# The output projection of a fused retention and SwiGLU kernel as seven products of halves, with its weight blocks streamed from DRAM

## The chip, the cores and the metric

One core of a Trainium2 chip runs the whole kernel. The metric is the device time of one execution, in microseconds. Where two kernels are compared by a ratio, it is the mean time of the one kernel's runs over the mean time of the other's runs of the same rounds on the same chip. It is therefore not quite the ratio of the medians that are quoted beside it.

The engines are called by the names of the profile: PE is TensorE (matmuls), PEld its weight loads, DVE is VectorE, ACT is ScalarE, POOL is GpSimd. SP is SyncE, which here does nothing but issue DMA transfers; SPq is its queue.

## The reference, cut to what matters

```python
# q, k, v: (8, 8, 576, 64).  Attention with decay, then, per token (4608 of them, 512 wide):
x   = ret(q, k, v)                                   # (4608, 512)
xn  = x / sqrt(mean(x*x) + 1e-6) * rms_g
g   = xn @ w_gate                                    # 512 -> 1536
val = xn @ w_val
out = (g * sigmoid(g) * val) @ w_out                 # 1536 -> 512, float32
```

The last product, with `w_out`, is the output projection, and it is what the change rewrites.

## The kernel before

The tokens are worked through in 12 tiles of 384 (`u` = 0 to 11). Tiles 0 and 1 belong to a start phase, in which the weights are also brought into float32. From tile 2 on, each tile consists of six steps of `up` (the two up projections, already written as seven products of halves, a Strassen scheme), then the output projection `down`. Attention for later tiles ("slots") and the norm of the next tile stand between them.

```python
    def down(u, s):                       # three times a tile, 128 tokens each
        ps = bank(f"out_{u}_{s}")
        for f in range(NF):               # 12 blocks of d_ff
            nc.tensor.matmul(
                ps[:, :DM], lhsT=h_of[u][:, f, s * P : s * P + P], rhs=w_out[:, f],
                start=(f == 0), stop=(f == NF - 1),
            )
        o = o_all[:, (u * (NS) + s) % 2]
        nc.scalar.copy(out=o, in_=ps[:, :DM])
        nc.sync.dma_start(out=out[u * U + s * P : u * U + s * P + P, :], in_=o)
    ...
    SLOTS = (((0, 2, 4, 5), 5), ((6,), 9), ((1, 3, 5), 10))

    def behind(u, i):                     # a slot, and the three steps of the next tile's norm
        at, n = SLOTS[u % 3]
        if i in at:
            j = u // 3 * 8 + n + at.index(i)
            slot(j)
            following(j)                  # transposes for j+1, then 13 loads for j+2
        if u + 1 < NU and 5 <= i < 8:
            (norm_0, norm_1, norm_2)[i - 5](u + 1)

    with tc.manual_schedule():            # every engine keeps this program order
        start()                           # ends with: down(0, s) and norm_s(2) in turn, slot(9)
        for u in range(2, NU):
            for i in range(2 * NG):
                for _ in up(u, i % 2, i // 2):
                    pass
                behind(u, i)
            for s in range(NS):
                down(u, s)
                behind(u, 2 * NG + s)
```

The last step of the norm, `norm_2`, scales x, and then forms four differences of quarters of x for the seven products:

```python
        for o, a, b in ((t3, b22, b12), (b12, b12, b11), (t2, b22, b12), (t4, b21, t2)):
            nc.vector.tensor_tensor(out=o, in0=a, in1=b, op=ALU.subtract)
```

Of the kernel before, what the change touches and what calls it, by code (L numbers as in the profile page):

```python
# [10 lines left out]
F32 = mybir.dt.float32  # L11
U32 = mybir.dt.uint32
AF = mybir.ActivationFunctionType
ALU = mybir.AluOpType
P = 128
# [27 lines left out]
def kernel(  # L43
# [11 lines left out]
    nc = tc.nc  # L55
    B, H, S, D = q.shape
    NTOK, DM = out.shape
# [6 lines left out]
    SQ = 32  # L64
    U = 384
    HU = U // 2
    NS = U // P
    NU = NTOK // U
    NH = NF // 2
    NG = NH // 2  # L70
# [5 lines left out]
    const = ctx.enter_context(tc.tile_pool(name="const", bufs=1))  # L76
# [2 lines left out]
    xp = ctx.enter_context(tc.tile_pool(name="xp", bufs=3))  # L79
    ffn = ctx.enter_context(tc.tile_pool(name="ffn", bufs=1))  # L80
    tmp = ctx.enter_context(tc.tile_pool(name="tmp", bufs=6))
    PS = bass.MemoryType.PSUM
    trio = ctx.enter_context(tc.tile_pool(name="trio", bufs=1, space=PS))
    banks = ctx.enter_context(tc.tile_pool(name="banks", bufs=5, space=PS))

    def bank(name):
        return banks.tile([P, 512], F32, tag="b", name=name)

    def temp(name):
        return tmp.tile([P, U], F32, tag="t", name=name)  # L90
# [17 lines left out]
    tick = const.tile([1, 1], F32, name="tick")  # L108
    rms_g = const.tile([P, NHP], F32, name="rms_g")
    w_out = const.tile([P, NF, DM], F32, name="w_out")  # L110
    o_all = const.tile([P, 2, DM], F32, name="o_all")



# [5 lines left out]
    A11, A12, S1, A22, S2, S3, S4 = range(7)  # L120
# [6 lines left out]
    x_of, t_of, h_of = {}, {}, {}  # L127
# [3 lines left out]
    def load_qk(j):  # L131
        b, hp = jobs[j]
        for nm, src in (("q", q), ("k", k)):

            t = raw.tile([P, S // SQ, SQ], F32, tag=nm + "raw", name=f"{nm}raw_{j}")
            for e in range(2):
                rows = src[b, 2 * hp + e].rearrange("(t b) (i a) -> i b t a", b=SQ, a=SQ)
                for i in range(D // SQ):
                    r = e * D + i * SQ
                    nc.sync.dma_start(out=t[r : r + SQ], in_=rows[i])  # L140
            st[j][nm + "raw"] = t
# [20 lines left out]
    def load_kv(j):  # L162

        b, hp = jobs[j]
        for nm, src, bufs in (("k", k, 4), ("v", v, 3)):
            if nm in st[j]:
                continue
            t = raw.tile([P, NFULL, 2, D], F32, tag=nm, name=f"{nm}_{j}", bufs=bufs)
            for e in range(2):
                nc.sync.dma_start(  # L170
                    out=t[:, :, e],
                    in_=src[b, 2 * hp + e, : NFULL * P].rearrange("(c p) d -> p c d", p=P),
                )
            st[j][nm] = t
        t = st[j]["vt"] = raw.tile([L, 2, D], F32, tag="vt", name=f"vt_{j}", bufs=3)
        nc.sync.dma_start(
            out=t, in_=v[b, 2 * hp : 2 * hp + 2, NFULL * P :].rearrange("e p d -> p e d")
        )
# [22 lines left out]
    def prepare(j):  # L201

        d = st[j]
        for nm in ("q", "k"):
            t = att.tile([P, S], F32, tag=nm + "T", name=f"{nm}T_{j}")
            nc.vector.transpose(out=t, in_=d.pop(nm + "raw").rearrange("p t a -> p (t a)"))
            d[nm + "T"] = t
        scale_v(j)
# [143 lines left out]
    def following(j):  # L352
        if j + 1 < len(jobs):
            prepare(j + 1)
        if j + 2 < len(jobs):
            load_qk(j + 2)
            load_kv(j + 2)
# [140 lines left out]
    def down(u, s):  # L498
        ps = bank(f"out_{u}_{s}")
        for f in range(NF):  # L500
            nc.tensor.matmul(  # L501
                ps[:, :DM], lhsT=h_of[u][:, f, s * P : s * P + P], rhs=w_out[:, f],
                start=(f == 0), stop=(f == NF - 1),
            )
        o = o_all[:, (u * (NS) + s) % 2]
        nc.scalar.copy(out=o, in_=ps[:, :DM])  # L506
        nc.sync.dma_start(out=out[u * U + s * P : u * U + s * P + P, :], in_=o)



    chunks = []
    for g in range(NG):
        for m, src in enumerate((moe_w_gate, moe_w_val)):
            for half in range(2):
                n = (half * NH + 2 * g) * P
# [87 lines left out]
    def combine(m):  # L603
        for g in range(NG):
            w = w_up[m][:, :, 2 * g * P : 2 * g * P + 2 * P]
            for o, a, b, op in (
                (S3, A11, A21, ALU.subtract), (S1, A21, A22, ALU.add),
                (S2, S1, A11, ALU.subtract), (S4, A12, S2, ALU.subtract),
            ):
                o, a, b = (w[:, 2 * n : 2 * n + 2] for n in (o, a, b))  # L610
                nc.gpsimd.tensor_tensor(out=o, in0=a, in1=b, op=op)

    def weights_to(n):

        nonlocal n_chunks
        while n_chunks < min(n, len(chunks)):
            mantissa(n_chunks + 1)
            join(n_chunks)
            load_chunks(n_chunks + 4)
            exponent(n_chunks + 2)  # L620
            n_chunks += 1
# [3 lines left out]
    def start():  # L625

        h_of[0] = ffn.tile([P, NF, U], F32, tag="h", name="h_0")
        tables = list(zip((causal, gv, gc, gq), (_causal_table(), *_decay_tables(H, D))))

        def table(i):  # L630
            t, values_ = tables[i]
            src = nc.inline_tensor(values_, name=t.tensor.name + "_table")
            nc.scalar.dma_start(out=t, in_=src.ap())

        make_identity(nc, ident)
        nc.vector.memset(ones, 1.0)
        for j in range(NHP):
            load_first(j)
            if j + 1 < NHP:
                load_kv(j)  # L640
        for i in (1, 0, 2):
            table(i)
        load_chunks(2)
        table(3)
        nc.scalar.dma_start(out=rms_g, in_=moe_rms_g.rearrange("(c p) -> p c", p=P))
        load_chunks(3)
        turn(0)
        sq = []
        for j in range(NHP):
            slot(j)  # L650
            if j + 1 < NHP:
                turn(j + 1)
            if j:
                sq.append(square(0, j - 1))
            if j == 0:
                exponent(0)
                exponent(1)
            elif j == 1:
                load_kv(NHP - 1)
                mantissa(0)  # L660
                weights_to(1)
                load_qk(NHP)
            elif j == 2:
                weights_to(2)
                load_kv(NHP)
        values(NHP - 1)
        carried(NHP - 1)
        sq.append(square(0, NHP - 1))
        norm_0(0, sq)
        norm_1(0)  # L670
        norm_2(0)
        following(NHP - 1)
        step = 0
        order = [(0, 0, 0), 4, (0, 1, 0), 5, (0, 0, 1), 6, (0, 1, 1), 7, (0, 0, 2)]
        order += [(1, 0, 0), (1, 1, 0), (0, 1, 2)]
        order += [(1, m, g) for g in (1, 2) for m in range(2)]
        for what in order:
            if not isinstance(what, tuple):
                slot(what, rest=what > NHP)
                following(what)  # L680
                if what == 2 * NHP - 1:
                    values(what)
                    carried(what)
                    norm_0(1)
                    norm_1(1)
                continue
            u, m, g = what
            weights_to(4 * g + 2 * m + 2)
            for _ in up_plain(u, m, g):
                step += 1  # L690
                weights_to(2 + (step + 1) // 2)
            if what == (0, 0, 2):
                norm_2(1)
        weights_to(len(chunks))
        combine(0)
        for u in (1, 0):
            for s in range(NS):
                down(u, s)
                if u == 0:
                    (norm_0, norm_1, norm_2)[s](2)  # L700
            if u:
                combine(1)
                slot(8, rest=False)
                following(8)
        slot(9)
        following(9)



    SLOTS = (((0, 2, 4, 5), 5), ((6,), 9), ((1, 3, 5), 10))  # L710

    def behind(u, i):
        at, n = SLOTS[u % 3]
        if i in at:
            j = u // 3 * 8 + n + at.index(i)
            slot(j)
            following(j)
        if u + 1 < NU and 5 <= i < 8:
            (norm_0, norm_1, norm_2)[i - 5](u + 1)

    with tc.manual_schedule():
        start()
        for u in range(2, NU):
            for i in range(2 * NG):
                for _ in up(u, i % 2, i // 2):
                    pass
                behind(u, i)
            for s in range(NS):
                down(u, s)
                behind(u, 2 * NG + s)  # L730


# [25 lines left out]
```

## Time and profile before

| | before |
|---|---|
| median of the first 3 runs | 1227.73 us (1227.61 to 1229.58) |
| span of the profiled run | 1226.5 us, granted clock 0.986 |
| TensorE busy | 1175.6 us, 96% |
| VectorE busy | 567.0 us, 46% |
| output projection on TensorE, one tile | 72 instructions of 512 columns, 30.9 us |
| one tile from the end of `up` to the next `up` (u=2) | 35.0 us, without a hole |

The page gives the totals. The chain of work that ended last says which of them count, and the timeline of one stretch, read engine by engine, says why. The prediction below shows those lines and how they are read.

### The profile page before, as it was taken

The numbers are of one execution on the slowest core, as the hardware profiler recorded it, in microseconds if no ns is written. First come the engines' busy times: TensorE is split into PE (matmuls) and PEld (weight loads), VectorE is DVE, ScalarE is ACT, GpSimd is POOL, SyncE is SP. The second block draws the span as 40 slices with busy tenths as digits, with TensorE's granted clock in tenths as the row PEclk, the third lists the DMA queues.
The fourth block names the chain that finished last, engine by engine and source line by source line (L and its number), as shares of the span: only waits on it lengthen the run. The fifth ranks groups of instructions, "written<-read, shape, count | busy, mean of one in ns | idle before, by whom it ended". The sixth has DMA issues, their size and how long they took to land.

```text
span 1226.5 us, 21417 instructions
## 1 busy us (share of the span) xinstructions
PE 1175.6 (96%) x9224; PEld 894.6 (73%) x9224; DVE 567.0 (46%) x1216; ACT 257.5 (21%) x488; POOL 45.2 (4%) x74
## 2 busy tenths in 40 slices
PE   4697899999999999999999999999999999999998
PEld 3455555447976985976985994985994995894993
DVE  3888871024643662433562663343563463342340
ACT  4554550012111120121220211211220220120110
POOL 0000004130000000000000000000000000000000
PEclk9799799999999999999999999999999999999999
DMA  8588420022240331002221242002122200000000
GB/s 219 118 209 202 122 99 1 18 64 47 44 80 18 62 72 46 1 9 56 39 51 51 40 76 55 9 1 59 33 50 55 47 2 18 9 1 18 9 1 26
DMA packets 224526, 65.52 MB, mean 53 GB/s; under 512 B 212016, under 2 KB 212144, under 8 KB 224432
## 3 DMA queue, kind: packets, MB, share of 16 engines
q1 hardware_dynamic: 215360, 45.12, 18.0%
q10 hardware_dynamic: 9072, 19.05, 4.7%
q8 instruction: 72, 1.18, 0.4%
q14 instruction: 22, 0.18, 0.0%
HBM read 54.70 MB, written 9.44 MB: 52 GB/s over the span
## 4 chain that ended last, share of the span: by engine, by line
PE 87%; DVE 1%; ACT 0%; issue 0%; POOL 0%; ACTq 0%; DVEq 0%; POOLq 0%
PE out L501 30%; PE x L430 13%; PE z L430 13%; PE w L430 13%; PE y L430 6%; PE up L487 6%; PE av L316 2%; PE av L297 1%; PE s L235 1%; PE s L255 1%; PE rb L397 1%; PE ms L377 0%; DVE x L399 0%; DVE w_val L597 0%; DVE sum L280 0%
## 5 line engine op out<-in xcount | busy, mean ns | idle before, releaser
L501 PE MATMUL out<-w_out,h 128*128 128x512 f32 x792 | 346.3, 594 | 0.0
L501 PEld LDWEIGHTS out<-w_out,h 128*128 128x128 f32 x792 | 149.0, 190 | 177.9 <-issue 175.1
L437 DVE TENSOR_TENSOR u<-m,y 128x384 f32<-128x384 f32 x60 | 32.7, 545 | 141.4 <-PE y L430 141.4
L506 ACT COPY o_all<-out 128x512 f32<-128x512 f32 x36 | 21.1, 586 | 366.3 <-PE out L501 348.4
L430 PE MATMUL z<-x,w_gate 128*128 128x192 f32 x480 | 87.9, 326 | 2.2 <-DVE sum L280 2.2
L430 PE MATMUL x<-x,w_val 128*128 128x192 f32 x480 | 88.8, 328 | 0.0
L430 PE MATMUL x<-x,w_gate 128*128 128x192 f32 x480 | 88.5, 328 | 0.0
L430 PE MATMUL w<-sums,w_gate 128*128 128x192 f32 x480 | 87.8, 326 | 0.0
L430 PE MATMUL z<-x,w_val 128*128 128x192 f32 x480 | 87.8, 326 | 0.0
L430 PE MATMUL w<-sums,w_val 128*128 128x192 f32 x480 | 87.8, 326 | 0.0
L430 PEld LDWEIGHTS x<-x,w_gate 128*128 128x128 f32 x480 | 79.5, 190 | 4.8 <-issue 4.3
L430 PEld LDWEIGHTS z<-x,w_gate 128*128 128x128 f32 x480 | 79.6, 190 | 2.5 <-DVE sum L280 2.5
L430 PEld LDWEIGHTS w<-sums,w_val 128*128 128x128 f32 x480 | 79.7, 190 | 0.0
L430 PEld LDWEIGHTS w<-sums,w_gate 128*128 128x128 f32 x480 | 79.7, 190 | 0.0
L430 PEld LDWEIGHTS z<-x,w_val 128*128 128x128 f32 x480 | 79.6, 190 | 0.0
L430 PEld LDWEIGHTS x<-x,w_val 128*128 128x128 f32 x480 | 79.2, 190 | 0.6
L454 ACT COPY m<-x 128x384 f32<-128x384 f32 x60 | 28.7, 479 | 202.9 <-PE x L430 202.9
L487 PE MATMUL up<-x,w_gate 128*128 128x384 f32 x192 | 68.3, 515 | 3.2 <-DVE x L399 1.5
L437 DVE TENSOR_TENSOR h<-u,w 128x384 f32<-128x384 f32 x60 | 33.3, 554 | 76.4 <-PE w L430 76.4
L268 DVE SCALAR_TENSOR_TENSOR ret<-s,causal 128x320 f32<-128x320 f32 x64 | 28.4, 486 | 86.8 <-PE last L255 49.8
L399 DVE SCALAR_TENSOR_TENSOR x<-x,rms_g,rb 128x384 f32<-128x384 f32 x48 | 26.3, 610 | 86.6 <-PE rb L397 86.6
L449 ACT ACTIVATE h<-h 128x384 f32<-128x384 f32 x90 | 47.0, 523 | 88.6 <-DVE h L437 88.6
(99 smaller groups left out, 1332.7 us busy)
## 6 DMA issues: line engine op xcount, KB each, us to landing
out_dram<-o_all SPq DMA_DIRECT2D x36, 256.0 KB, 2.0
k<-in_k_dram SPq DMA_DIRECT2D x64, 128.0 KB, 3.0
v<-in_v_dram SPq DMA_DIRECT2D x64, 128.0 KB, 2.8
qraw<-in_q_dram SPq DMA_DIRECT2D x112, 72.0 KB, 2.5
kraw<-in_k_dram SPq DMA_DIRECT2D x112, 72.0 KB, 2.6
w_out<-in_moe_w_gate_dram ACTq DMA_DIRECT2D x6, 1024.0 KB, 6.8
w_out<-in_moe_w_val_dram ACTq DMA_DIRECT2D x3, 1024.0 KB, 5.7
w_gate<-in_moe_w_val_dram ACTq DMA_DIRECT2D x3, 1024.0 KB, 6.1
```

What stands on the lines that cost most here:

```text
L235: nc.tensor.matmul(s[side(odd), e, i * L : i * L + L], lhsT=d["kT"][side(e), c * L : c * L + L], rhs=d["qT"][side(e), c * L : c * L + L], ...
L255: nc.tensor.matmul(o[side(e)], lhsT=d["k"][side(odd), i, e], rhs=d["v"][side(odd), i, e], start=True, stop=True,)
L268: nc.vector.scalar_tensor_tensor(out=ret[:, e], in0=s[:, e, :SC].rearrange("p (c k) -> p c k", k=L), scalar=float(_gamma(H)[2 * hp + e] ** ...
L316: mm = nc.tensor.matmul(av[odd][side(e), i * L : i * L + L], lhsT=d["sum"][side(e), c - 1], rhs=d["qT"][side(e), c * L : c * L + L], start ...
L399: nc.vector.scalar_tensor_tensor(out=x[:, c], in0=x[:, c], scalar=rms_g[:, c : c + 1], in1=rb[:, :U], op0=ALU.mult, op1=ALU.mult,)
L430: nc.tensor.matmul(ps[:, i * HU : i * HU + HU], lhsT=w_up[m][:, 2 * blk + c, cut], rhs=t_of[u][blk][:, c], start=(start and i == c == 0), ...
L437: nc.vector.tensor_tensor(out=o, in0=a, in1=pairs_of(ps), op=ALU.add)
L449: nc.scalar.activation(out=o, in_=c, func=AF.Silu)
L454: nc.scalar.copy(out=s1, in_=pairs_of(x_))
L487: nc.tensor.matmul(ps[:, :U], lhsT=w_up[m][:, 4 * half + c, i * P : i * P + P], rhs=x_of[u][:, c], start=(c == 0), stop=(c == NHP - 1),)
L501: nc.tensor.matmul(ps[:, :DM], lhsT=h_of[u][:, f, s * P : s * P + P], rhs=w_out[:, f], start=(f == 0), stop=(f == NF - 1),)
L506: nc.scalar.copy(out=o, in_=ps[:, :DM])
```

## The change

The intent is to save an eighth of the output projection's TensorE work. With d_model on the output partitions, the product of a 512x1536 and a 1536x384 matrix is cut into halves each way, and seven products of halves replace eight. This needs sums of blocks of `w_out` (formed once, on GpSimd), sums of blocks of h (four on VectorE for each tile), seven weight blocks where the tile of `w_out` holds four (so all seven are kept in DRAM and streamed through four slots), and a transposition of the results on the way out (VectorE, in 32x32 blocks; each result then leaves in eight stores with rows of 128 bytes).

```diff
+    w_blocks = dram.tile([7, P, NH, DH], F32, name="w_blocks")
+    w_slots = w_out.rearrange("p f d -> p (f d)").rearrange("p (s f d) -> p s f d", s=4, d=DH)
...
+    def combine_out():
+        a11, a12, a21, a22 = (quarter(r, c) for r in range(2) for c in range(2))
+        for o, a, b, op in (
+            (a22, a21, a22, ALU.add), (a21, a11, a21, ALU.subtract),
+            (a11, a22, a11, ALU.subtract), (a12, a12, a11, ALU.subtract),
+        ):
+            nc.gpsimd.tensor_tensor(out=o, in0=a, in1=b, op=op)
...
+    def fetch():                          # one block from DRAM into the slot that came free
+            nc.sync.dma_start(
+                out=w_slots[:, n_fetched % 4], in_=w_blocks[ORDER[n_fetched % 7]]
+            )
...
+    def across(u):
...
+        def product(rhs, ps, start):      # 12 matmuls of 192 columns, then a fetch
...
+        block(t1, b12, b11, ALU.subtract)
+        block(b12, b22, b12, ALU.subtract)
+        yield                             # the slot and norm_0 stand here
+        product(b11, x_, True)
+        ...
+        yield
+        product(t1, z, True)
+        yield                             # norm_1 here
+        product(b12, w, True)
+        yield
+        product(b11, y, True)
+        add(u2, s1, y); add(u4, u2, z); result(1, 1, u4, w)
+        yield                             # norm_2 here
+        product(b21, x_, False); result(0, 0, None, x_); block(b21, b21, b11, ALU.subtract)
+        yield
+        product(b22, z, False);  result(0, 1, u2, z)
+        yield
+        product(b21, w, False);  result(1, 0, u2, w)
...
         slot(9)
         following(9)
+        return combine_out()
-    SLOTS = (((0, 2, 4, 5), 5), ((6,), 9), ((1, 3, 5), 10))
+    SLOTS = (((0, 2, 4, 5), 5), ((5,), 9), ((1, 3, 5), 10))
```

The stores of the four sums and the first four fetches are issued behind the third `up` step of tile 2. Tiles 0 and 1 keep `down`.

More of the change, by code (lines that the diff above doesn't have):

```diff
@@ L81 @@
     tmp = ctx.enter_context(tc.tile_pool(name="tmp", bufs=6))
+    outs = ctx.enter_context(tc.tile_pool(name="outs", bufs=3))
     PS = bass.MemoryType.PSUM
+    dram = ctx.enter_context(tc.tile_pool(name="dram", bufs=1, space=bass.MemoryType.DRAM))
     trio = ctx.enter_context(tc.tile_pool(name="trio", bufs=1, space=PS))
@@ L110 @@
     w_out = const.tile([P, NF, DM], F32, name="w_out")
-    o_all = const.tile([P, 2, DM], F32, name="o_all")
     A11, A12, S1, A22, S2, S3, S4 = range(7)
@@ L504, in down, with quarter @@
             )
-        o = o_all[:, (u * (NS) + s) % 2]
+        o = outs.tile([P, DM], F32, tag="o", name=f"o_{u}_{s}")
         nc.scalar.copy(out=o, in_=ps[:, :DM])
         nc.sync.dma_start(out=out[u * U + s * P : u * U + s * P + P, :], in_=o)
+    ORDER = (A11, S1, S3, S2, A12, S4, A22)
+    DH = DM // 2
+    w_blocks = dram.tile([7, P, NH, DH], F32, name="w_blocks")
+    w_slots = w_out.rearrange("p f d -> p (f d)").rearrange("p (s f d) -> p s f d", s=4, d=DH)
+    n_fetched = 0
+    def quarter(row, col):
+        return w_out[:, col * NH : col * NH + NH, row * DH : row * DH + DH]
@@ new lines, in keep @@
+    def keep(blk, t):
+        nc.sync.dma_start(out=w_blocks[blk], in_=t)
+    def combine_out():
[5 more added lines that the diff above has]
+            nc.gpsimd.tensor_tensor(out=o, in0=a, in1=b, op=op)
+        return (S1, a22), (S3, a21), (S2, a11), (S4, a12)
+    def fetch():
+        nonlocal n_fetched
+        if n_fetched < 7 * (NU - 2):
+            nc.sync.dma_start(
+                out=w_slots[:, n_fetched % 4], in_=w_blocks[ORDER[n_fetched % 7]]
+            )
+            n_fetched += 1
@@ new lines, in across, with add, block, result @@
+    def across(u):
+        h = h_of[u]
+        b11, b12 = h[:, :NH, :HU], h[:, :NH, HU:]
+        b21, b22 = h[:, NH:, :HU], h[:, NH:, HU:]
+        t1 = ffn.tile([P, NH, HU], F32, tag="t1", name=f"t1_{u}")
+        x_, y, z, w = (bank(f"{n}o_{u}") for n in "xyzw")
+        s1, u2, u4 = (temp(f"{n}o_{u}") for n in ("m1", "u2", "u4"))
+        def product(rhs, ps, start):
+            k = 7 * (u - 2) + n_done
+            for i in range(2):
+                for c in range(NH):
+                    nc.tensor.matmul(
+                        ps[:, i * HU : i * HU + HU],
+                        lhsT=w_slots[:, k % 4, c, i * P : i * P + P], rhs=rhs[:, c],
+                        start=(start and i == c == 0), stop=False, skip_group_check=True,
+                    )
+            fetch()
+        def add(o, a, ps):
+            nc.vector.tensor_tensor(out=o, in0=a, in1=ps[:, :U], op=ALU.add)
+        def block(o, a, b, op):
+            nc.vector.tensor_tensor(out=o, in0=a, in1=b, op=op)
+        def result(row, col, a, ps):
+            r = ps[:, :U]
+            if a is not None:
+                r = temp(f"c{row}{col}_{u}")
+                add(r, a, ps)
+            o = outs.tile([P, DM], F32, tag="o", name=f"o_{u}_{row}_{col}")[:, :U]
+            nc.vector.transpose(out=o, in_=r)
+            o = o.rearrange("p (d t r) -> p d t r", d=2, r=SQ)
+            for d in range(2):
+                for i in range(P // SQ):
+                    c0 = row * DH + d * P + i * SQ
+                    t0 = u * U + col * HU
+                    nc.sync.dma_start(
+                        out=out[t0 : t0 + HU, c0 : c0 + SQ].rearrange("(t c) r -> c t r", c=SQ),
+                        in_=o[i * SQ : i * SQ + SQ, d],
+                    )
+        n_done = 0
+        block(t1, b12, b11, ALU.subtract)
+        block(b12, b22, b12, ALU.subtract)
+        yield
+        product(b11, x_, True)
+        nc.scalar.copy(out=s1, in_=x_[:, :U])
+        block(b11, b12, b11, ALU.add)
+        n_done += 1
+        yield
+        product(t1, z, True)
+        n_done += 1
+        yield
+        product(b12, w, True)
+        n_done += 1
+        yield
+        product(b11, y, True)
+        add(u2, s1, y)
+        add(u4, u2, z)
+        result(1, 1, u4, w)
+        n_done += 1
+        yield
+        product(b21, x_, False)
+        result(0, 0, None, x_)
+        block(b21, b21, b11, ALU.subtract)
+        n_done += 1
+        yield
+        product(b22, z, False)
+        result(0, 1, u2, z)
+        n_done += 1
+        yield
+        product(b21, w, False)
+        result(1, 0, u2, w)
+        yield
@@ L694, in start @@
         weights_to(len(chunks))
+        for blk, row, col in ((A11, 0, 0), (A12, 0, 1), (A22, 1, 1)):
+            keep(blk, quarter(row, col))
         combine(0)
@@ L717, in behind @@
             following(j)
-        if u + 1 < NU and 5 <= i < 8:
+        if u + 1 < NU and i >= 5:
             (norm_0, norm_1, norm_2)[i - 5](u + 1)
     with tc.manual_schedule():
-        start()
+        kept = start()
         for u in range(2, NU):
@@ L726 @@
                     pass
+                if u == 2 and i == 2:
+                    for blk, t in kept:
+                        keep(blk, t)
+                    for _ in range(4):
+                        fetch()
+                if i == 2 * NG - 1:
+                    rest = across(u)
+                    next(rest)
                 behind(u, i)
-            for s in range(NS):
-                down(u, s)
-                behind(u, 2 * NG + s)
+            for i, _ in enumerate(rest):
+                if i in (1, 3):
+                    behind(u, 6 + i // 2)
 _INS = ['q', 'k', 'v', 'moe_w_gate', 'moe_w_val', 'moe_w_out', 'moe_rms_g']
```

## The prediction

Where a cut is marked, a statement about the hardware, or a calculation with one, is gone that was not taken from this case's traces. The duration of a block sum of 1152 elements (1.35 us: 5.4 us for four and 2.7 for two, and from these the shift of 2.05 us) came from a formula. It can be estimated from the trace of the kernel before as well: a VectorE TENSOR_TENSOR took 348 ns for 192 elements (L331) and 554 ns for 384 (L437), or 1.07 ns for each further element, which makes about 1.38 us for 1152.

> **What bounds the kernel now.** I read the page's totals first, then the chain of work that ended last, then the groups of instructions.
>
> ```profile
> PE 1175.6 (96%) x9224; PEld 894.6 (73%) x9224; DVE 567.0 (46%) x1216; ACT 257.5 (21%) x488; POOL 45.2 (4%) x74
> ...
> L501 PE MATMUL out<-w_out,h 128*128 128x512 f32 x792 | 346.3, 594 | 0.0
> ...
> L430 PE MATMUL w<-sums,w_val 128*128 128x192 f32 x480 | 87.8, 326 | 0.0
> ```
>
> TensorE is busy 96% of the span, and its matmul groups have no idle time in front of them, so TensorE sets the time. The chain by line gives "out L501" 30%: that is the output projection, which the change rewrites. The mean of one instruction (594, 326 ns) overstates it, because matmuls overlap. The chain in order of time shows what they really occupy:
>
> ```profile
> 348.42 1.30 PE w L430 x8
> 352.42 10.50 PE out L501 x24
> 363.48 10.41 PE out L501 x24
> 374.54 10.30 PE out L501 x24
> 384.84 1.30 PE x L430 x8
> ```
>
> Two instructions of the trace make one fp32 matmul of the program (24 for 12). So 512 columns cost 10.30/24 = 0.429 us an instruction, and 192 columns 1.30/8 = 0.1625 us. The up projection already works as seven products of 192 columns and shows that this form runs back to back at the full rate, weight loads hidden. This is tile u=2 of 12 (384 tokens each): up ends at 349.65, the attention slot takes until 352.35, and three "down" groups with two short norm matmul groups between them run until 384.67, without a hole.
>
> The neighbours in that stretch, by engine, from the timeline:
>
> ```profile
> 351.55 0.89 DVE L268 SCALAR_TENSOR_TENSOR ret<-s,causal 128x320 f32<-128x320 f32 x2 [0.64 <-PE s L255]
> ...
> 356.98 1.58 DVE L370 TENSOR_TENSOR sq<-sq,sq 128x384 f32<-128x384 f32 x3
> ```
>
> ```profile
> 356.42 1.96 SPq L140 DMA_DIRECT2D qraw<-in_q_dram  x4
> 358.48 2.06 SPq L140 DMA_DIRECT2D kraw<-in_k_dram  x4
> ...
> 362.84 0.61 SPq L176 DMA_DIRECT2D vt<-in_v_dram  x1
> ```
>
> VectorE finishes the sums for the next norm at 358.56, long before TensorE asks for them (362.76). SyncE needs 7.05 us to issue 13 loads, 0.49 us for each small one.
>
> [...] SyncE waits 293 us in all for VectorE's transposes before it loads into their buffers. [...] by windows (DMA share, GB/s last):
>
> ```profile
> 120.00:122.00 2.00, 0.00 (x0) 0.00 (x0) 2.00 (x2) 0.00 (x0) 0.00 (x0) 1.00 0.94 266
> ...
> 358.50:360.50 2.00, 2.00 (x6) 0.92 (x5) 0.06 (x1) 0.00 (x0) 0.00 (x0) 1.00 0.85 137
> ...
> 364.50:366.00 1.50, 1.50 (x4) 0.57 (x3) 0.68 (x3) 0.00 (x0) 0.12 (x1) 1.00 0.52 186
> ```
>
> Rows of 2 KB move at 266 GB/s, the 128-byte rows of q and k at 137; and a slot's loads are not drained until about 365.3, some 2 us after the last issue.
>
> **The change, part by part.** Ten tiles (u=2 to 11) change; u=0 and 1 keep the old form.
>
> *TensorE, removed and added.* Removed 72 x 0.429 = 30.9 us a tile. Added 7 products x 2 halves x 6 blocks x 2 instructions = 168 x 0.1625 = 27.3 us (3.9 us a product). Gain 3.6 us a tile, 36.0 us in all. This is wholly on the path.
>
> *VectorE, added.* A tile gets four block sums of 1152 elements (5.4 us), five adds (2.8) and four transposes of 384 elements (scaling 0.75 us for 576: about 0.55 each, 2.2): 10.4 us a tile, 104 in all, to 671 us (55%). No bound as a total, but it is in order, and its place counts. Let T be the end of the up products (349.65). Two of the sums (2.7 us) come before the slot's work. VectorE is then free for "ret" at about T+3.95 instead of T+1.9, and all behind it shifts by 2.05 us: the norm's sums end at T+11.0. TensorE now reaches the norm's matmuls after two products, at T+2.7+7.8 = T+10.5, no longer after 10.3 us of "down". It waits 0.5 us. That holds for the seven tiles whose sixth step has a full slot (u=2 to 8): +3.5 us.
>
> *The weight stream.* Seven blocks of 786 KB per tile go through four slots; block k+4 may be fetched when product k has ended, on SyncE's queue. Four lie ready at the start. In program order the slot's 13 loads stand before the first fetch, and they wait for the transposes, so they now run from T+8.85 to T+15.9. The fetch that product 0 freed at T+6.6 is issued only then. The loads are drained at T+17.7 (365.3 shifted by 2.05); 786 KB at 266 GB/s take 3.0 us; and 1 MB issued in the quiet took 4.8 us to land against 3.9 at that rate, so 0.9 us more: T+21.6. Product 4 wants it at T+2.7 + 4x3.9 + 0.5 + two norm groups of 0.65 = T+20.1. Wait 1.5 us. The next two fetches follow 3.0 us apart, and the products need 3.9: no more waits. Seven tiles: +10.5 us. Tiles 9 to 11 have no such loads.
>
> *Late block sum.* The sum for product 6 stands behind the norm's eight operations (4.5 us) and a transpose; I get T+28.35 against T+27.9 where the fetch did not already delay TensorE (u=9, 10): +1 us together.
>
> *Tail.* Before, the last matmul is followed by one copy and one store:
>
> ```profile
> 1222.43 0.59 ACT L506 COPY o_all<-out 128x512 f32<-128x512 f32 x1 [9.76 <-PE out L501]
> 1223.04 0.33 SPq L507 DMA_DIRECT2D out_dram<-o_all  x1
> ```
>
> 4.2 us from 1222.3 to the end. Now each of four results leaves in 8 stores of 24 KB with 128-byte rows, at an issue cost near 0.49 us: 3.9 us each, as long as a product. They queue: counted from the start of the last tile's first product, products end at 27.3, SyncE starts the last result at 29.7, issues its last store at 33.1, and 3.5 us later all has landed (as before: 1223.04 to 1226.5). Tail 9.3, so +5 us.
>
> *Start.* Storing seven blocks and the four GpSimd sums (1536 elements at 1.33 us per 512: 4 us each) run beside tile u=2's up products (57 us); the first fetches should be there some 10 us early. I count 0.
>
> Sum: 1227.7 - 36.0 + 3.5 + 10.5 + 1.0 + 5.0 = 1211.7 us.
>
> **Rivals.** (1) *All hidden*: only the tail and the norm wait remain: 1227.7 - 36 + 5 + 3.5 = 1200. For it: TensorE is gapless today and the fetches have a nominal lead of three products. Against it: SyncE's program order. (2) *The stream is the bound*: fetches at 137 GB/s instead of 266 (5.7 us each) would outlast the 3.9 us products; three fetches each tile then cost some 4 + 2 + 2 us, and ten tiles eat the gain twice over: 1240 and more. Against it: 6 KB rows, like the wide rows that ran at 266. (3) *Banks*: across a tile four accumulators live in five PSUM banks beside the slot's three and the norm's one. If a product or norm matmul must wait for the slot's banks (freed by VectorE near T+8), that is up to 5 us in seven tiles: about 1245. Against it: today's "down" starts right after the same slot with no hole. (4) *VectorE as bound*: 55% leaves it out as a total.
>
> **Range and chances.** The gain of 36 us rests on two measured rates and is nearly certain. The debit of 20 us is built of margins of 0.5 to 1.5 us, each of which may vanish or double; waits that I overlooked pull one way only. Range 1200 to 1224. The 2% line lies at 1203.2, near rival 1: faster 0.2; within 2% 0.74; slower (rivals 2 and 3, above 1252) 0.06.
>
> **What would show it.** Right: 168 matmul instructions of 128x192 a tile, 3.9 us a product; TensorE idle before product 4 of u=2 to 8, released by a DMA into the weight slots, whose issue stands right behind the v loads; a short wait before the norm's matmuls, released by VectorE's sums; a last store some 9 us after the last matmul. Wrong: no idle time in front of product 4 (then rival 1), waits before most products released by DMA (2), or waits before a product released by VectorE's reads of the slot's banks (3); and products longer than 3.9 us would undo the gain itself.

## The result, and the profile after

| | before | after |
|---|---|---|
| median (4 runs each, same rounds) | 1227.89 us | 1223.18 us (1222.38 to 1223.73) |
| ratio | | 0.9958 (95%: 0.9941 to 0.9976) |
| span, granted clock | 1226.5 us, 0.986 | 1222.0 us, 0.974 |
| TensorE busy | 1175.6 us, 96% | 1150.0 us, 94% |
| VectorE busy | 567.0 us, 46% | 676.9 us, 55% |

The kernel is 4.7 us faster. The forecast of 1211.7 us with a range down from 1224.0 held the time just inside its range, but the gain came out at less than a third of the 16 us that were forecast. The totals of the page already say where to look: TensorE does less work than before, as intended, but has holes now.

```profile
PE 1150.0 (94%) x10184; PEld 1036.6 (85%) x10184; DVE 676.9 (55%) x1346; ACT 244.1 (20%) x468; POOL 59.7 (5%) x78
```

The view of who waited for whom, cut to TensorE from 283 us on (where tile 2 begins), lists every wait. The columns are the total in us, the number of waits, and the longest one. In the same stretch the kernel before has one wait of 2.2 us and one of 0.3.

```profile
PE y L432 <- DVE sums L412: 8.1, 1, 8.1
PE xo L557 <- DMA w_out<-w_blocks: 6.8, 7, 2.3
PE z L432 <- DVE sum L282: 4.0, 1, 4.0
PE ms L379 <- DVE sq L372: 1.4, 7, 0.2
PE wo L557 <- DVE h L568: 0.5, 2, 0.2
PE av L318 <- POOL tick L307: 0.3, 1, 0.3
```

The second, fourth and fifth lines are the waits that the prediction named: the fifth product waits for its block in seven tiles, the norm's matmuls for VectorE in seven, the last product for the late block sum in two. The sixth was there before. The first line is none of them. It is the largest wait of the kernel, it happens once, and it lies in the `up` projection, which the change doesn't touch. The third line (2.2 us before) lies right behind it.

First the part that was foreseen. This is TensorE in tile 2 of the changed kernel, from the fourth product to the next tile's `up`:

```profile
377.69 4.06 PE L557 MATMUL yo<-h,w_out 128*128 128x192 f32 x24
381.59 0.81 PE L399 MATMUL rb<-diag,ones 128*128 128x384 f32 x2
384.67 5.82 PE L557 MATMUL xo<-h,w_out 128*128 128x192 f32 x24 [2.27 <-DMA w_out<-w_blocks]
390.32 4.06 PE L557 MATMUL zo<-h,w_out 128*128 128x192 f32 x24
```

From 377.69 to 381.59 is 3.90 us for one product, as computed. The fifth product should start at 382.24 and starts at 384.67, and then takes 5.65 us, because the clock granted fell to 0.53 and 0.62 in the two windows of 2 us that follow (PEclk is the column third from the end, GB/s the last):

```profile
384.60:386.60 2.00, 1.93 (x6) 1.96 (x7) 1.97 (x5) 0.00 (x0) 0.00 (x0) 0.53 1.02 427
386.60:388.60 2.00, 2.00 (x9) 2.00 (x9) 1.90 (x4) 0.00 (x0) 0.00 (x0) 0.62 1.00 390
```

SyncE's queue in that tile shows why the block was late; the first fetches stand right behind the last of the loads:

```profile
378.51 0.65 SPq L178 DMA_DIRECT2D vt<-in_v_dram  x1
379.25 2.85 SPq L538 DMA_DIRECT2D w_out<-w_blocks  x4
```

Now the part that was not foreseen: the start of tile 2. VectorE in the kernel before, with the four differences of `norm_2`:

```profile
286.05 0.56 DVE L410 TENSOR_TENSOR sums<-x 128x384 f32<-128x384 f32 x1
286.64 0.56 DVE L410 TENSOR_TENSOR x<-x 128x384 f32<-128x384 f32 x1
287.23 0.56 DVE L410 TENSOR_TENSOR sums<-x 128x384 f32<-128x384 f32 x1
287.82 0.56 DVE L410 TENSOR_TENSOR sums<-x,sums 128x384 f32<-128x384 f32 x1
```

The same work in the changed kernel, and the scaling of x ahead of it:

```profile
282.89 2.19 DVE L401 SCALAR_TENSOR_TENSOR x<-x,rms_g,rb 128x384 f32<-128x384 f32 x4 [9.24 <-PE rb L399]
285.11 2.58 DVE L412 TENSOR_TENSOR sums<-x 128x384 f32<-128x384 f32 x1
287.73 3.65 DVE L412 TENSOR_TENSOR x<-x 128x384 f32<-128x384 f32 x1
291.42 3.66 DVE L412 TENSOR_TENSOR sums<-x 128x384 f32<-128x384 f32 x1
295.11 3.66 DVE L412 TENSOR_TENSOR sums<-x,sums 128x384 f32<-128x384 f32 x1
```

And GpSimd, at the same time, with the block sums that the change added:

```profile
283.83 14.52 POOL L532 TENSOR_TENSOR w_out<-w_out 128x1536 f32<-128x1536 f32 x4
```

The reader should see three things. The four differences take 2.58 to 3.66 us instead of 0.56, and 3.66 is what one GpSimd sum takes (14.52/4 = 3.63). The four scalings ahead of them, which have one input in PSUM, take 2.19 us for four as before, although GpSimd works during the second half of them. And as soon as GpSimd is done, VectorE is back at its old durations. TensorE's second product of tile 2 needs the third of these differences (t2), which ends at 295.08:

```profile
295.13 2.93 PE L432 MATMUL y<-sums,w_gate 128*128 128x192 f32 x8 [8.08 <-DVE sums L412]
```

The fourth holds up VectorE's work for attention behind it, and so TensorE's third product, which waits the 4.0 us.

The start of tile 2 can be measured as the step from its preceding slot to the end of its `up` products: 65.94 us before (283.71 to 349.65), 79.29 us after (282.78 to 362.07). That is 13.35 us lost. The two waits make 8.1 + 4.0 - 2.2 = 9.9 of it (the 2.2 was there before), and the rest, about 3.5, is clock. The windows of the changed kernel show it in the column PEclk:

```profile
287.00:295.10 8.10, 0.06 (x1) 0.00 (x0) 8.01 (x3) 0.48 (x1) 7.87 (x4) 0.63 0.00 0
295.10:297.80 2.70, 2.67 (x8) 2.42 (x8) 2.69 (x1) 0.00 (x0) 2.70 (x1) 0.50 0.00 0
...
302.00:304.80 2.80, 2.76 (x9) 2.76 (x10) 2.63 (x7) 0.00 (x0) 0.00 (x0) 0.50 0.06 10
```

TensorE idles for 8.08 us, the clock granted behind that is 0.50, and the products that follow take longer: the third 2.72 us (302.04 to 304.76), where it took 1.40 before (291.65 to 293.05).

### The profile page after: what moved, and what is told of

Its sections match the earlier page's. It is cut to its first block, busy times and chain, and to the rows that moved or that the text cites. A ratio compares the mean times of both kernels' runs of the same rounds, so it can differ in the third digit from the quotient of the medians.

```text
span 1222.0 us, 24026 instructions
## 1 busy us (share of the span) xinstructions
PE 1150.0 (94%) x10184; PEld 1036.6 (85%) x10184; DVE 676.9 (55%) x1346; ACT 244.1 (20%) x468; POOL 59.7 (5%) x78
## 4 chain that ended last, share of the span: by engine, by line
PE 74%; DVE 9%; DMA 3%; SPq 1%; issue 1%; ACT 0%; DVEq 0%; POOL 0%; POOLq 0%
PE x L432 13%; PE z L432 13%; PE w L432 13%; PE y L432 6%; PE up L489 6%; PE wo L557 6%; PE out L503 5%; PE xo L557 4%; PE zo L557 4%; DMA w_out<-w_blocks 3%; DVE sum L282 1%; PE av L318 1%; DVE h L568 1%; PE yo L557 1%; DVE sums L412 1%; PE av L299 1%
## 5 line engine op out<-in xcount | busy, mean ns | idle before, releaser
L557 PE MATMUL xo<-h,w_out 128*128 128x192 f32 x480 | 84.3, 333 | 6.8 <-DMA w_out<-w_blocks 6.8
L557 PEld LDWEIGHTS xo<-h,w_out 128*128 128x128 f32 x480 | 79.5, 193 | 12.0 <-issue 10.9
L557 PE MATMUL wo<-h,w_out 128*128 128x192 f32 x480 | 82.3, 328 | 0.5 <-DVE h L568 0.5
L557 PEld LDWEIGHTS wo<-h,w_out 128*128 128x128 f32 x480 | 77.9, 190 | 1.1 <-DVE h L568 1.1
L489 PEld LDWEIGHTS up<-x,w_gate 128*128 128x128 f32 x192 | 37.9, 200 | 32.6 <-issue 4.9
L489 PE MATMUL up<-x,w_val 128*128 128x384 f32 x192 | 65.0, 499 | 0.0
```

Source lines behind the costliest of these rows:

```text
L489: nc.tensor.matmul(ps[:, :U], lhsT=w_up[m][:, 4 * half + c, i * P : i * P + P], rhs=x_of[u][:, c], start=(c == 0), stop=(c == NHP - 1),)
L557: nc.tensor.matmul(ps[:, i * HU : i * HU + HU], lhsT=w_slots[:, k % 4, c, i * P : i * P + P], rhs=rhs[:, c], start=(start and i == c == 0) ...
```

## The experiments

Two theories stood against each other for the 13 us. Theory A says that VectorE instructions with two SBUF inputs wait for GpSimd instructions that read SBUF. The trace above suggests it: beside the sums the four differences, whose two inputs both lie in SBUF, took up to 3.66 us instead of 0.56, and the four scalings, with one input in PSUM, 2.19 us as before. Theory B says that the stores of the blocks, the first fetches or VectorE's load hold tile 2 up. A third question was whether the waits for the weight blocks have the cause that the prediction gave. The first four experiments ran in one call, the last three in another, each beside the kernel before on the same chip (medians of before 1229.62 and 1229.76 us there). All seven results were correct. Differences between experiments of different calls are taken from the ratios, times 1227.9 us.

**e1: the sums on VectorE.** In eight pieces, one behind each product from the fourth product of tile 2 on.

```diff
-            nc.gpsimd.tensor_tensor(out=o, in0=a, in1=b, op=op)
+            for c in (0, NH // 2):
+                o_, a_, b_ = (t[:, c : c + NH // 2] for t in (o, a, b))
+                nc.vector.tensor_tensor(out=o_, in0=a_, in1=b_, op=op)
+                yield
...
```

> The changed kernel with the four block sums of the output weights taken from GpSimd (4 x 3.63 us) to VectorE, in eight pieces of 768 elements (about 1 us each by 0.554 us for 384 plus their excess), one behind each product from the fourth product of tile 2 on. Theory A (VectorE's norm sums of tile 2 stood behind GpSimd's sums: 3.66 us each where they take 0.56): the step from the slot before tile 2 to the end of its up products goes back from 79.3 to about 66 to 67 us, and the kernel to about 1210 us (1208 to 1213). Rival B (it is the seven stores of the blocks and the first fetches, or VectorE's load, that hold up tile 2): 1219 us or more.

Measured: 1209.1 us (1206.96 to 1213.76), ratio 0.9838 (0.9814 to 0.9862). Against the changed kernel's 0.9958 that is 14.7 us less. The start of tile 2 takes 65.94 us (284.76 to 350.70), exactly as before the change, though VectorE now does 7.6 us of sums in addition. VectorE's timeline of e1 has the differences at their old duration:

```profile
288.27 0.56 DVE L412 TENSOR_TENSOR sums<-x 128x384 f32<-128x384 f32 x1
288.87 0.56 DVE L412 TENSOR_TENSOR sums<-x,sums 128x384 f32<-128x384 f32 x1
```

Stores and fetches are all still there, and VectorE does the sums in addition, so theory B falls for this step.

**e2: the same GpSimd work in smaller instructions.** Each of the four sums becomes six of 256 elements.

```diff
-            nc.gpsimd.tensor_tensor(out=o, in0=a, in1=b, op=op)
+            for c in range(NH):
+                nc.gpsimd.tensor_tensor(out=o[:, c], in0=a[:, c], in1=b[:, c], op=op)
```

A1 and A2 are two readings of theory A: by A1 a VectorE instruction waits for the one GpSimd instruction that is running, by A2 it is slowed for as long as GpSimd works at all.

> The changed kernel with each GpSimd sum cut into six instructions of 256 elements, the same work in all. Theory A1 [...]: each VectorE operation with two SBUF inputs waits for at most one piece, some 0.6 us, so tile 2 is late by some 3 us and not 13.4: about 1212 to 1214 us. Theory A2 (they share it in proportion as long as GpSimd works): as late as before, 1221 to 1224 us. Rival B: 1223 us.

Measured: 1212.1 us (1211.58 to 1213.3), ratio 0.9859 (0.9843 to 0.9876), 12.2 us less than the changed kernel. The start of tile 2 takes 69.43 us, so 3.5 of the 13.35 us remain. VectorE's and GpSimd's timelines of e2:

```profile
287.50 0.97 DVE L412 TENSOR_TENSOR sums<-x 128x384 f32<-128x384 f32 x1
...
283.95 17.72 POOL L533 TENSOR_TENSOR w_out<-w_out 128x256 f32<-128x256 f32 x24
```

GpSimd now works longer in all (17.72 us against 14.52), and yet VectorE is held up far less: 0.41 us an operation (0.97 - 0.56), within the 0.74 us of one GpSimd piece (17.72/24). Here the delay goes with the length of one GpSimd instruction, 0.41 us beside 0.74 and 3.10 (3.66 - 0.56) beside 3.63, and not with GpSimd's total. That is what A1 expected; a proportional sharing (A2) falls.

**e3: the kernel before with the sums added.** Four GpSimd sums read `w_out` at the same place and write to a buffer that nobody reads.

```diff
         slot(9)
         following(9)
...
+        for a, b in ((a21, a22), (a11, a21), (a22, a11), (a12, a11)):
+            nc.gpsimd.tensor_tensor(out=o, in0=a, in1=b, op=ALU.add)
```

> The kernel before, plus four GpSimd sums of 1536 elements at the same place, read from the output weights and written to a buffer that nobody reads: the disputed cost by itself, without stores, fetches or products. Theory A: late by 13 us in tile 2, 1241 us (1238 to 1243), with VectorE's norm sums of tile 2 at some 3.6 us each. Rival B: 1228 us, since GpSimd is idle there anyway.

Measured: 1242.35 us (1240.98 to 1243.72), ratio 1.0103 (1.0088 to 1.0118). The start of tile 2 takes 79.61 us, 13.67 more than before, with the same waits of 8.1 and 4.0 us and the differences at 3.65 us:

```profile
PE y L430 <- DVE sums L410: 8.1, 1, 8.1
```

Four instructions of an engine that stood idle, on data that nobody uses, cost the old kernel 1%. The sums alone bring the whole loss back.

**e6: the kernel before with GpSimd writes only.** In place of the sums, ten instructions that fill the same buffer and read nothing.

```diff
+        for n in range(10):
+            nc.gpsimd.memset(o, 0.0)
```

> The kernel before, plus ten GpSimd instructions at the place of the sums that only write 1536 elements of SBUF and read nothing. Theory A [...]: VectorE's norm sums stay at 0.56 us, 1228 to 1230 us. Rival (any GpSimd work on SBUF, or the issue of GpSimd's instructions, holds VectorE): the norm sums are slowed again and the kernel is at 1232 us or more.

Measured: 1229.1 us median of 2 runs, ratio 0.9996 (0.9978 to 1.0014). VectorE's and GpSimd's timelines of e6:

```profile
287.70 0.56 DVE L410 TENSOR_TENSOR sums<-x,sums 128x384 f32<-128x384 f32 x1
...
284.50 14.30 POOL L712 MEMSET scratch<- 128x1536 f32 x10
```

GpSimd is busy for as long as in e3 (14.30 us against 14.52), and VectorE's differences take 0.56 us, where they took 3.65 in e3. So in these runs it is GpSimd's instructions that read SBUF that hold VectorE, not its being busy or its writing.

**e4: the loads behind the fetches.** For the slot beside the output projection, the 13 loads of q, k and v are issued behind the fetch of the third product.

```diff
             slot(j)
-            following(j)
+            following(j, now=(i < 5))     # at step 5: the transposes only
+            if i == 5:
+                late.append(j)
...
             for i, _ in enumerate(rest):
+                if i == 2 and late:
+                    following(late.pop(), now=None)      # the loads
```

> The changed kernel with the 13 loads of q, k and v of the slot beside each output projection put behind the fetch of the third product on SyncE's queue. Theory of the prediction (the first fetch stands behind the loads): the waits before the fifth product (0.4 to 2.4 us in seven tiles, 8.0 in all, and 1.75 us of slower clock behind the longest) vanish, the late block sum then shows in seven more tiles at about 0.4 us: some 7 us less, 1216 us (1214 to 1218). Rival (the transfers themselves are too slow, because reads of w_blocks compete with 128-byte rows): the waits stay or move, 1221 us or more.

Measured: 1217.41 us (1216.63 to 1219.77), ratio 0.9904 (0.9888 to 0.9919), 6.6 us less than the changed kernel. The waits for weight blocks are gone from the list of waits. In their place stands the late block sum, now in nine tiles:

```profile
PE wo L557 <- DVE h L568: 2.1, 9, 0.2
```

In tile 2 the first fetch now goes out at 369.38, 6.9 us behind the end of `up` (362.48), where it was 17.2 us. So the fetches were late because of their place in SyncE's program order, and the transfers themselves keep up with the products.

**e5: the last stores on two queues.** Every second store of the last tile is issued by ScalarE.

```diff
-                    nc.sync.dma_start(
+                    q_ = nc.scalar if u == NU - 1 and i % 2 else nc.sync
+                    q_.dma_start(
```

> The changed kernel with every second store of the last tile issued by ScalarE instead of SyncE. Theory of the prediction (the tail of 9.0 us after the last matmul is made of issues of 0.49 us one behind the other): eight issues become four and four side by side, and the results no longer queue: the tail falls to about 6.5 us, 2.5 us less, 1220.7 us. Rival (it is the landing of 128-byte rows in DRAM that takes the time): the tail stays at 8.5 to 9 us.

Measured: 1222.01 us (1219.88 to 1223.33), ratio 0.9934 (0.9920 to 0.9947). By times alone this is inconclusive, since its interval overlaps that of the changed kernel. The trace settles the tail. The last product starts at 1210.61 and so ends at 1214.51, and the span is 1220.0: 5.5 us, where the changed kernel has 9.0 (1209.13 + 3.90 = 1213.03, to 1222.0). I expected 6.5. The stores of the last tile, in the changed kernel and on SyncE's half in e5:

```profile
1203.97 15.77 SPq L582 DMA_DIRECT2D out_dram<-o  x32
...
1205.45 12.24 SPq L583 DMA_DIRECT2D out_dram<-o  x16
```

**e7: all four together.** e1, e4 and e5, and the norm's last two steps one product later (behind the third and fifth product).

```diff
-                if i in (1, 3):
-                    behind(u, 6 + i // 2)
+                if i in (2, 4):
+                    behind(u, 5 + i // 2)
```

> The changed kernel with all repairs: sums on VectorE, late loads, the norm's two steps one product later (behind the third and fifth product and not the second and fourth), last stores on two queues. If the terms add: 13.4 (start) + 9.0 (fetch waits with clock) + 2.6 (norm waits) + 0.8 (late block sum) + 2.5 (tail) = 28 us under the changed kernel: 1195 us (1193 to 1199), and over 2% faster than the kernel before. Rival (VectorE, with the sums and the transposes, becomes the next bound): 1203 us or more.

Measured: 1195.07 us (1193.93 to 1196.98), ratio 0.9721 (0.9707 to 0.9734): 2.8% faster than the kernel before, which makes it the best of all kernels here. TensorE's waits from tile 2 on are down to the two that the kernel before had:

```profile
PE z L432 <- DVE sum L282: 2.2, 1, 2.2
PE av L318 <- POOL tick L307: 0.3, 1, 0.3
```

VectorE is busy for 56% of this span, and the only wait on it that is left is the 2.2 us of the kernel before.

## Why the prediction was right or wrong

The prediction's sum can be held against the trace term by term.

| term | predicted, us | measured, us | measured how |
|---|---|---|---|
| products | -36.0 | -36.0 | last tile: 27.30 from the first product to the end of the seventh, against 30.90; ten tiles |
| norm's wait | +3.5 | +2.6 | 0.37 in each of seven tiles |
| wait for weight blocks | +10.5 | +9.7 | seven waits before the fifth product, 0.37 to 2.43, sum 7.98; and 1.75 of slower clock in tile 2 |
| late block sum | +1.0 | +0.8 | 0.39 in tiles 9 and 10 |
| tail | +5.0 | +4.7 | 9.0 after the last product, 4.3 before |
| start | 0 | +13.35 | 79.29 against 65.94 |
| sum | -16.0 | -4.85 | the spans differ by -4.5 |

**Wrong: one step.** It is the sentence "Storing seven blocks and the four GpSimd sums (1536 elements at 1.33 us per 512: 4 us each) run beside tile u=2's up products (57 us) ... I count 0." The duration was about right (3.63 us), and so was the statement that there was time enough. What failed is "beside". The prediction checked the sums against the time at which their results were needed, but not against what else ran on VectorE at that moment. They fell on the four two-input operations of the norm, which TensorE was about to wait for. e3 shows that this step alone costs 13 us, and e1 that the changed kernel without it takes 1209 us, with 1211.7 forecast. The other half of the sentence, the stores and the first fetches at 0, held: e1 keeps them, and its start takes 65.94 us. None of the four rivals named the step either: rival 4 looked at VectorE's total only. So it is luck that the time lies inside the range: a term from outside the working nearly used up the room above the forecast. The other terms as measured give 1227.7 - 18.2 = 1209.5 us.

**Right: the saving.** One product takes 3.90 us, and 168 instructions of 192 columns run back to back wherever their data is there. A column costs the same in both forms: 0.429 us for 512 and 0.1625 us for 192 are 0.84 and 0.85 ns each.

**Right: the order on SyncE's queue.** The fetch that product 0 freed was forecast at T+15.9, T being the end of the `up` products. In tile 5 of the changed kernel it is issued at 657.88, which is 15.8 us behind the start of the slot (17.2 in tile 2). e4 shows the cause by undoing it.

**Mis-sized: the wait for weight blocks.** The wait was forecast at 1.5 us in each of seven tiles and is between 0.37 and 2.43. Why tiles 2 and 5 wait longest isn't settled. In tile 2 one of the loads ahead was itself issued 1.3 us late, but in tile 5 the loads went out without a gap, and the block took 6.2 us to land instead of the median 4.9. The rate of 266 GB/s, taken from rows of 2 KB, was too low: the four blocks fetched together in tile 2 landed some 2 us apart (3.0 forecast), and the two windows above moved 427 and 390 GB/s, the first stores of results included. The lower clock behind the longest wait was not forecast: 2.27 us of idle time in tile 2 were followed by a granted clock of 0.53 and 0.62 and a product of 5.65 us, and 1.97 us at the same place in e1 by a product of 5.66 us. But 1.87 us in tile 5 of the changed kernel were followed by a product of 3.97 us, and 2.24 us in tile 2 of the kernel before by 1.40 us for 8 instructions. So the length of a gap alone doesn't decide here, and what does is not measured.

**Right: norm's wait, late sum and tail**, within 1 us each. The rivals "the stream is the bound" and "banks" found no trace: no product but the fifth waits for a block, and none waits for a bank.

## What to carry to other kernels

Work that is moved to an idle engine is not free for that reason alone: here four GpSimd sums, on an engine that stood idle, cost 13 us. Before counting such work as 0, look at what the critical chain runs at that very moment, and whether those are VectorE instructions with two SBUF inputs while GpSimd reads SBUF (3.66 us instead of 0.56 here). If the work has to stay there, cut it into short instructions: with pieces of 0.74 us the same differences took 0.97 us, and the kernel 12.2 us less. On SyncE's queue, which issues in program order, put the transfer that the bottleneck needs next ahead of those that are needed only later, even if the latter can go earlier (6.6 us in e4). The long run of small stores at the end gained from a second queue here: the last 32 stores of 24 KB, issued by SyncE alone in 15.77 us, left 9.0 us behind the last matmul, and issued by SyncE and ScalarE 5.5.
